# A conformer block on one core: every background matmul moved into the attention's 64x64 tiles

## The chip, the cores and the metric

The kernel runs on one core of a Trainium2 chip. The metric is the device time of one execution in microseconds. Its profile comes from one further execution, taken by the hardware profiler. The engines are PE (TensorE), ACT (ScalarE), DVE (VectorE), POOL (GpSimd) and SP (SyncE, which here only issues DMAs).

## The reference

Two sequences of 4000 tokens with 144 features pass through one conformer block: a feed-forward layer with residual, attention with 4 heads of 36 features, a gated convolution over 5 tokens, a second feed-forward layer and a last layer norm. All inputs and the output are bfloat16.

```python
h = _silu(_layernorm(x) @ w_ff1a) @ w_ff1b          # 144 -> 576 -> 144
x = x + 0.5 * h
qkv = _layernorm(x) @ w_qkv                         # 144 -> 432, 4 heads of 36
p = _softmax(einsum('bhqd,bhkd->bhqk', q, k) * 36 ** -0.5)
x = x + einsum('bhqk,bhkd->bhqd', p, v) @ w_o
h = _layernorm(x) @ w_pw1                           # 144 -> 288
h = h[..., :144] * _sigmoid(h[..., 144:])
x = x + _silu(depthwise_conv5(h, dw)) @ w_pw2
x = x + 0.5 * (_silu(_layernorm(x) @ w_ff2a) @ w_ff2b)
return _layernorm(x)
```

## The kernel before

**Work and tiles.** The 8000 tokens are 16 chunks of 500 (8 for each sequence), a chunk is four blocks of 125 tokens. Attention goes over phases (a chunk of queries) and key tiles of 64: 1008 pairs of chunk and tile for the four heads. For each pair four QK matmuls fill the array at once (64 rows x 64 columns each: the two heads of a pair on the two partition halves, the two pairs side by side) and write 2 x 500 columns in two PSUM banks. The exponential turns them into probabilities PT: on ACT in one instruction of 1000 columns, or, for 190 of the pairs, on DVE in five instructions ("DVE tile"). Four PV matmuls (64 rows x 37 columns; the 37th column sums the probabilities) add into PSUM banks 6 and 7. QK and PV matmuls are all in tiles of 64x64.

**Background.** Everything else is called background and runs between the attention's instructions: layer norms (statistics on DVE, power and scaling on POOL), transposes of a normalized chunk (through DRAM by DMA, from `XN` to `rows` to `XT` or `XTQ`; in the head and the tail on PE), the feed-forward layers (`ff`, `ff_tile`, `ff_part`, weights `WA`, `WE`, `WB`), projections to Q, K and V (`proj`, `vproj`), the output projection (`WO`), the gate (`glu`, `glu_left`, weights `WP1`, `WPZ`), the convolution as matmuls with diagonal matrices (`conv`, `DG`) and its projection (`WP2`). These matmuls use the whole array: 144 features are 128 rows and a second slice of 16 rows padded to 80 (72 and 72 for `XTQ`). Outside the tail silu is computed as tanh on ACT (tile `TH`) and a product on DVE, so that the exponential's table can stay loaded.

**Banks.** Banks 0 to 5 serve QK pairs and the background, one bank at a time for the background; 6 and 7 collect PV.

**What sets the order.** A recording layer (`Rec`, `Sched`) writes all instructions down engine by engine. Generators stand for the chains of background work; `pick` chooses what comes next by costs and due times (`POLICY`, one value for every 21 pairs). After that `reorder` shifts blocks of each engine by a table (`ORDER`), and `PLACES` gives the PSUM banks. What is left is a fixed order on every engine, with semaphore waits. Matmuls carry a `kind` ("q" for the attention's tiles, "f" for full ones); the planner charges a fixed time where the kind changes. In the head, where PE would pause, `Rec.op` inserts matmuls on the identity matrix (`warm`, as many as `FILLS` says) beside the 50 at the start.

**Head and tail.** In the head chunk 0 is taken in two halves (`pre_first`) with weights loaded from ACT's and SP's queues; the last three chunks are finished after the last exponential (`mode["tail"]`), again in halves, with the silu table loaded.

The helper that issues every instruction is at line 419, so all rows of the profile name L419 and are told apart by their tiles.

Of the kernel before, what the change touches and what calls it, by code (L numbers as in the profile page):

```python
# [12 lines left out]
D = 144  # L13
H = 4
DH = 36
HD = 72
ML = 128
LC = 16
LP = 80
# [5 lines left out]
CW = 502  # L25
# [9 lines left out]
FILLS = (5, 2, 5, 12, 3, 1, 3) + (0,) * 60  # L35

# [3 lines left out]
        "PPPPPPPPQOPPPPROQNPPQRPQLPPRPTPUPNIZOVOKVVL~OOKOK~OUHINSNLMMMOPNOJSOOL[I[KMYMKOGRNJHFKOOOE^NNN_dMKLM"  # L40
        "nXMJ@LJMFMYGaJNKMJhLLLLljKKKKKKWKMMWNKK`BJJJQRecHFSIGKH]QKMRGKPMJJMMQTNPNXTRSUJUJJJSLPMPPQUQQNKOTOOR"
        "OQLPPPPPYOOPN[NNNOMfRNLYULMIMOS^KIMOJNaNNQMNHPPaUOMQNYKPSPPQUSVV^QQ^_Q5<@QCPMKIMNNTQMSMNSNUOYQKMMOQQ"
        "^MSOORNOPPCOORPZP^O]OOO[OCNOQEHMUJNNTOMR[MQWXMPMMNNDMPXSNNZMMTMMMTMPLMPP]OOOOQQNUKNOMQMP]WNOMPNVKYPN"
        "JNQHNOOPQQQMPPQOPUP]MNNNOOTNNOMNWOPPMPNOW]VNN[MMHMKYMMQ]YKI`JLQYJJKV[KHMJTLJOJPMQORPVMQNYMN]MN[bLLLL"
        "LMNLPRPKWOYFMNOVNOHXXMKOLNNNN[[_MMMTLLTKKKLJOOPRP`MO_OMNOMPQLLMRMMMPPPQOSYP[MOOISOLNPPIPSPTOLRNNWPNO"
        "QQMMPUQRN[QQQRJFPPPPJQQSPPKQQNPPPPVPPQOPVXOOPNDNPRROSVSYNFWMPYUPNDPJFPNPTOPYOLOPNQ[NLNRPMRLNNOPhUNZM"
        "MMNLNNPMMWYLPNZKNLMF[LPPSLVINLNOMWQNYPYPLQHKOSNORPGPPPS[OOLOOPPYLNNNVOMNOM^QMNTOO_KMMNOMPPLPNQOYL]RY"
        "LMKLMMPLY]KLNNQXMRXSLI[MDObNOENPMMNSNNQMMWNNNOSVNiKZNNQOTFNNOMXXUMMMM?TLLIYMQXXLLMMQZMJJ`ORLMUMKQYNL"
        "INPMMUVNLNOMYPMOORNNRUNKPNO_ROQLSSKMQMKPROLPSOORNOSOOOTVNNNNSNTMTMNNOVXNOMORLSNVXIMSYLMKLN^XYNLMNHMM"
        "WLLMXMNYMOLNNXMNXMMVMM[SLJLLZN^OLNNJUbLLLQNLPRGNNOOOPNRNOPPPeOOOOPSOOORROf`OPNO^@QDLJLMOLTKLTMTRKGMQ"  # L50
        "QNUOPNROYYPZOHNbILLLLbTLLSLLLLPLM_M[MMMMMcMMMMNLMOdZMNNNNIMMMMXMNNVOMKMMZNOUaMMMQMM]^HOMKNNNJZMKM[LM"
        "QgLLLMWMMMMU]LLLV^MQJMWTMHBHMZSKL[PLLZTMK_bMMIGbMPLPQMSVCKRKSMBINPPSPVOLOOOOZQNNS[MMMMNSMOMNO]aNNcMM"
        "MMMMMMNLNNNZWNZMZPNKPMYBENOPJYNNPMPQOLQNPPRRO[YQJNOPQOPXFPHPNOOOPWOOOOOOXPMTQOLOK^OXNNOMPPPLPPHQQNgR"
        "cOLQOMPNOOOOdRM@LdOJOIPIOOOJOOOOJOOPNUPNOOQQYLQ]NLZ[LLLdWKIKLLLWULE]LLLLLOMWRcKLLLNZM[PMMRILNKZJ`[JK"
        "MOLLUbKeJLLYKOUKMMMMMY=KMNNZNL^NLNNNNNN_NNNOQQNPTHNN_NLOOO^QMNPKO^QQM_JFPLOPJMNPPLPhMPROOPQOWOWNNNNU"
        "U?NO[HMTOOOCNOOOQO[OQOUOOOPHVORPYMGNPPMOVNN[QOVKPNZPGLOY]OPLOPPPBHOOORPRROR`OPWQNZCLNNPQZKMQETOJOMNU"
        "OOOOOPPPP[OOPNQNQRLMVZLOTNKPLLOOPPVPNOVOMRMOSLOOPPPPPZOWOMNNN]NLMPRTLNZUNLQMNYWNRAOPTOSHRNDQOPTOOPNP"
        "UOUQ_LROQQIQFNOYPNUKQNKTNKOQRSTNQNRXFQOQVQULMVEMPPP[PPPQODZcMPMMQINPKMPNOOOPRMNPPPQOZOOOOOQOMOOPXOOZ"
        "NNNNNN`NPWMXNNOPNKOCNOXPNOQOMZQMUOKXMZP[^XIMMOOKPABPJOPPPXOOQOPPPRIOPSOVSMOTKQUKLPNQNPXQOMROMPMQWQMU"
        "OQNJMQQNPQQTQOKTNO[NQOPQOUOOVRMUZPNVSYMN`OQK6TNNZ;NLNVMMMMTMMVWMMdMNLMNOO]N[MMM]XLJKKRK^aJHNPPRKNX>N"  # L60
        "OJLOMNPPPSPPQTVOOQVPLPQOAPQOPQOQZVOLOMRUMKL[MPMOOQWMMNNYOLNORNNNOYVNNNOWLMMROORROH]QNQMNOXNOMPMUPKMY"
        "NTOLORSTJMWOPPFObTYLNQSMKG_MKMNN`RMKLOLR]MKPNgIMMMNOYNKNNNNNZTMQXILIXJLMQLYOSJMNPU_]JLOKRSMMHLMOMQOW"
        "OOQOMOUNPNUQRM`YYLOREKNKKV[LJNLOSQJN`KPXLObLMWNK]MIJQLLOUO^LDLTKQNLVLQ^MMQRMSFMUWMNNWMG^MTRMJYLRPNGO"
# [2083 lines left out]
```

## Time and profile before

| | us |
|---|---|
| median of two runs | 875.17 (874.74 and 875.6) |
| span of the profiled execution | 873.9 |
| first exponential starts | 19.38 |
| silu table loaded for the tail | 838.61 |

The profiled execution's span runs from its first to its last instruction; what lies around it is not in it. Matmuls are pipelined, so PE's busy share counts each one's whole length through the array and is not a measure of how much more would fit. "Idle before" in a group's row is idle time of that engine just ahead of these instructions, with what ended it.

### The profile page before, as it was taken

To read this page: it belongs to the slowest core of one execution; us is meant where nothing else is said; L and a number is where in the kernel's file an instruction comes from. 1 tells how busy PE (TensorE), PEld (TensorE's weight loads), DVE (VectorE), ACT (ScalarE), POOL (GpSimd) and SP (SyncE) were. 2 spreads that over 40 slices of the span, in tenths; PEclk is the share of its full clock that TensorE was granted. 3 is DMA by queue.
4 is the path that set the end of the run, shared out by engine and by line. 5 is a ranking of instruction groups with operands and counts; after the bars stand their busy time and mean duration, and the time that the engine had idled before them with its cause. 6 is when DMAs were issued, how large, how long until landed. Compare 5 with 4: busy or idle time off the path is not lost.

```text
span 873.9 us, 27051 instructions
## 1 busy us (share of the span) xinstructions
PE 844.3 (97%) x11419; PEld 385.8 (44%) x11419; DVE 824.8 (94%) x1821; ACT 845.4 (97%) x1098; POOL 292.8 (34%) x573
## 2 busy tenths in 40 slices
PE   8999999999999999999999999999999999999996
PEld 6543444334444434443444444445444433444465
DVE  7988999999999999999989999899999999999987
ACT  6799999999999999999999999999999999999985
POOL 6750350341325141152211552621314413022434
PEclk9999999999999999999999999999999999999999
DMA  4230101121121020212001120110111011001111
GB/s 100 49 62 29 23 17 44 33 67 30 29 52 39 17 50 11 45 22 47 23 4 29 24 56 17 30 30 16 37 31 24 21 31 21 19 15 38 28 26 35
DMA packets 114353, 28.82 MB, mean 33 GB/s; under 512 B 101090, under 2 KB 114230, under 8 KB 114230
## 3 DMA queue, kind: packets, MB, share of 16 engines
q1 hardware_dynamic: 112646, 26.39, 13.8%
q8 instruction: 90, 1.47, 0.7%
q10 hardware_dynamic: 1584, 0.69, 0.3%
q14 instruction: 33, 0.27, 0.1%
HBM read 13.44 MB, written 13.61 MB: 31 GB/s over the span
## 4 chain that ended last, share of the span: by engine, by line
ACT 59%; PE 25%; DVE 11%; POOL 4%; issue 1%; POOLq 0%; DVEq 0%
ACT PT L419 54%; PE PS L419 25%; ACT TH L419 5%; DVE PT L419 4%; POOL XN L419 2%; POOL RS L419 2%; DVE ST L419 2%; DVE X L419 1%; DVE XN L419 1%; DVE HT L419 1%; DVE U L419 0%; DVE KT L419 0%; DVE RS L419 0%; DVE AN L419 0%; DVE XT L419 0%
## 5 line engine op out<-in xcount | busy, mean ns | idle before, releaser
L419 ACT ACTIVATE PT<-PS 128x1000 bf16<-128x1000 f32 (+1 forms) x818 | 752.0, 1051 | 3.7 <-PE PS L419 2.8
L419 PE MATMUL PS<-QT,KT 64*64 64x500 bf16 x3968 | 419.9, 384 | 12.4 <-ACT PT L419 7.4
L419 PE MATMUL PS<-PT,VA 64*37 64x500 bf16 x4728 | 406.4, 372 | 1.6 <-DVE QT L419 1.0
L419 DVE TENSOR_SCALAR PT<-PS 128x500 int16<-128x500 f32 x380 | 250.2, 668 | 6.9 <-PE PS L419 5.1
L419 PEld LDWEIGHTS PS<-QT,KT 64*64 64x64 bf16 x3968 | 124.8, 104 | 232.0 <-ACT PT L419 132.2
L419 POOL TENSOR_SCALAR RS<-ST 125x4 f32<-125x4 f32 x130 | 37.8, 291 | 475.6 <-DVE ST L419 469.0
L419 PEld LDWEIGHTS PS<-PT,VA 64*37 64x37 bf16 x4728 | 142.7, 96 | 93.4 <-issue 13.6
L419 DVE TENSOR_SCALAR PT<-PT 128x1000 uint16<-128x1000 uint16 x380 | 154.2, 419 | 2.3 <-PE PS L419 1.0
L419 POOL TENSOR_SCALAR XN<-X,RS 125x144 bf16<-125x144 bf16 x260 | 144.7, 586 | 9.7 <-DMA out_dram<-XN 1.5
L419 DVE TENSOR_TENSOR PT<-PT 128x1000 bf16<-128x1000 bf16 x190 | 127.5, 674 | 0.9
L419 ACT ACTIVATE TH<-PS 128x500 bf16<-128x500 f32 (+3 forms) x194 | 102.8, 551 | 4.7 <-PE PS L419 4.5
L419 POOL TENSOR_TENSOR RS<-RS,NHALF 125x4 f32<-125x4 f32 (+1 forms) x93 | 92.8, 1002 | 33.5 <-DVE RS L419 27.9
L419 DVE SCALAR_TENSOR_TENSOR HT<-TH,PS 128x500 bf16<-128x500 bf16 (+1 forms) x135 | 81.0, 613 | 10.1 <-ACT TH L419 9.7
L419 PE MATMUL PS<-XT,WA 80*128 80x500 bf16 (+5 forms) x288 | 74.5, 364 | 4.2 <-DVE XT L419 1.0
L419 DVE BATCH_NORM_STATS2 ST<-X 125x6 f32<-125x288 bf16 x160 | 65.5, 446 | 1.6 <-DMA X<-in_x_dram 1.4
L419 DVE SCALAR_TENSOR_TENSOR X<-PS,X 125x288 bf16<-125x288 f32 (+1 forms) x128 | 56.6, 449 | 5.6 <-PE PS L419 4.3
L419 PE MATMUL PS<-WB,HT 128*125 128x144 bf16 (+1 forms) x640 | 52.6, 230 | 0.8 <-ACT HT L419 0.5
L419 PEld LDWEIGHTS PS<-WB,HT 128*125 128x125 bf16 (+1 forms) x640 | 44.3, 136 | 14.2 <-issue 4.3
L419 PEld LDWEIGHTS PS<-XT,WA 128*128 128x128 bf16 (+1 forms) x288 | 21.1, 97 | 37.7 <-issue 10.1
L419 POOL COPY U<-U 128x2 bf16<-128x2 bf16 (+1 forms) x54 | 12.0, 263 | 56.2 <-DVE U L419 56.2
L419 DVE STREAM_TRANSPOSE XN<-XN 128x320 f32<-128x320 f32 x54 | 27.0, 500 | 2.8 <-POOL XN L419 2.6
L419 PE MATMUL PS<-U,DG 128*128 128x250 bf16 (+6 forms) x204 | 28.8, 263 | 0.1
(95 smaller groups left out, 519.9 us busy)
## 6 DMA issues: line engine op xcount, KB each, us to landing
rows<-XN SPq DMA_DIRECT2D x216, 40.0 KB, 2.0
XT<-rows SPq DMA_DIRECT2D x56, 128.0 KB, 2.0
rows<-AN SPq DMA_DIRECT2D x60, 40.0 KB, 2.0
X<-in_x_dram SPq DMA_DIRECT2D x15, 140.6 KB
XTQ<-rows SPq DMA_DIRECT2D x26, 70.3 KB
out_dram<-XN SPq DMA_DIRECT2D x13, 140.6 KB
XT<-rows SPq DMA_DIRECT2D x56, 16.0 KB, 1.9
out_dram<-XN SPq DMA_DIRECT2D x3, 70.3 KB
```

Of the source, the lines that this page charges most:

```text
L419: ins = getattr(eng, o.name)(*o.a, **o.k)
```

## The change

Every background matmul except three kinds (the float32 transposes of the attention's output, those with `KL`, and the warm-up) is written as matmuls of at most 64 rows and 64 output columns.

- **144 features are three slices of 48 rows**, and they lie twice in SBUF, on partitions 0 to 47 and 64 to 111 (`KS`, `NS`, `HF`). The two copies are the two lanes `r` of the array. Weights are loaded in that form: `load_a` and `load_b` issue two DMAs for each weight, `load_heads` loads `WQ` and `WK` head by head, eight DMAs, in place of one load of `WQKV` and copies on POOL. `WE`, `HT5` and most zero fills are gone.
- **Lanes and banks.** Lane 0 and lane 1 write into different banks (but for V and the leftover channels, where they share one). `Couple` and `Pair` take two banks at once. `residual` works on all four blocks of a chunk in one go (two blocks a lane), and one DVE instruction of 576 columns adds them to X in place of two of 288.
- **`lane_run`**: outside head and tail a background step of one lane (two matmuls) goes together with one half of a PV step on the other lane (`partner`, `emit_O`).
- **Transposes** on PE are done by halves of 64 columns (`spread`), three slices, and copied in one instruction of 750 columns for two blocks; by DMA they are read back twice, once for each partition half. `XTQ` is a ring of five chunks in place of eight.
- The fillers and `FILLS` are gone; the 50 matmuls at the start stay.
- `POLICY`, `FJ`, `ORDER` and `PLACES` have new values. 194 pairs go to DVE (190 before), 798 + 16 to ACT (802 + 16).

The core of the diff:

```diff
-LP = 80
+HF = 64
+KS = 48
+NS = 3
-FILLS = (5, 2, 5, 12, 3, 1, 3) + (0,) * 60
+def c_q(n, ways=4):
+    return (n / 2400 + 0.0028) / ways
...
-        if eng == "pe" and self.filler is not None and not self.filling:
...
+class Couple:
+    def take(self):
+        return self.banks.take(), self.banks.take()
...
+    def load_a(eng, q, W, wa, nm, lat=None):
+        for r in range(2):
+            n0, n1 = r * 5 * HF, min((r + 1) * 5 * HF, FF)
+            load(eng, q, W[HF * r:HF * r + KS, :, 0:n1 - n0], by_slice(wa)[:, :, n0:n1], [(nm, "a", r)], lat=lat)
...
-    load_ff("act", "w0", "w3", WA1, WE1, WB1, w_ff1a, w_ff1b, "W1", 3.5, 4.5)
-    load("act", "w1", WQKV[0:HD, :, :], kh(w_qkv), ["WQKV"], lat=5.0)
+    load_a("act", "w0", WA1, w_ff1a, "W1", 3.5)
+    load_b("act", "w3", WB1, w_ff1b, "W1", 4.5)
+    load_heads("act", "w1", WK, D, "WK", 5.0)
+    load_heads("act", "w1", WQ, 0, "WQ", 5.0)
...
+    def lane_run(r, steps, per):
+        for x in range(0, len(steps), per):
+            group = steps[x:x + per]
+            if x:
+                yield need("pe", dur=0.215, kind="q", hold=True)
+            m = None if alone() else partner(1 - r)
+            for y, quads in enumerate(group):
+                for out, l, rh, start, stop, rk, bk, cols in quads:
+                    op("pe", "matmul", out, lhsT=l, rhs=rh, start=start, stop=stop, ...)
+                if y == 0 and m is not None:
+                    emit_O(m, (1 - r,))
...
+        def mm(i, r, a, b):
+            j = i % 2 * TB
+            return [(HT[HF * r:HF * r + HF, h, t, j + a:j + min(b, TB)], WB[HF * r:HF * r + HF, t, :]) for t in range(9)]
+        yield from residual(c, range(NB), mm, 0.5 if silu else 0.25, [("HT", h), (nm, "b", 0), (nm, "b", 1)])
...
     "pe": (
-        "PPPPPPPPQOPPPPROQNPPQRPQLPPRPTPUPNIZOVOKVVL~OOKOK~OUHINSNLMMMOPNOJSOOL[I[KMYMKOGRNJHFKOOOE^NNN_dMKLM"
+        'PPPPPQSNOOPPPPPPQRNOPPPPPPPP`OOVOMXNLoLrKK~OSK^JJJLLLMOMIJLLPKKKMMM[LLRTJJLrHcIJbKKUKKKLQKKKFJMMJLgKPNLf[LMKfjJJJJ[J`IIIdHHIjHiJaFMGBFVGJPFi'
```

What the new order makes of two places. First PE in the middle, at the gate and the output projection of a chunk (WP and XT: the gate; WO and XT: the output projection; QT,KT and PT,VA: the attention's QK and PV). Before:

```order
L419 MATMUL PS<-PT,VA 37x500 x2
L419 MATMUL PS<-XT,WP 128x500 x2
L419 MATMUL PS<-QT,KT 64x500 x4
L419 MATMUL PS<-PT,VA 37x500 x4
L419 MATMUL PS<-QT,KT 64x500 x6
```

After:

```order
L388 MATMUL PS<-XT,WP 64x500 x2
L388 MATMUL PS<-PT,VA 37x500 x6
L388 MATMUL PS<-QT,KT 64x500 x4
L388 MATMUL PS<-PT,VA 37x500 x4
L388 MATMUL PS<-XT,WP 64x500 x2
L388 MATMUL PS<-PT,VA 37x500 x2
L388 MATMUL PS<-XT,WP 64x500 x2
L388 MATMUL PS<-PT,VA 37x500 x2
```

Two full matmuls on 128 columns stood in one run between attention matmuls; six on 64 columns now stand in three runs, each followed by PV matmuls, and the last two runs have PV matmuls between them.

Second ACT at the program's head (WA, WE, WB: weights of the first feed-forward layer; WQKV, WK, WQ, WV: of the projections; DUM: the first use of the loaded table; HT: silu). Before:

```order
L419 DMA WA<-in_w_ff1a_dram 128x512
L419 DMA WA<-in_w_ff1a_dram 16x512
L419 DMA WE<-in_w_ff1a_dram 128x64
L419 DMA WE<-in_w_ff1a_dram 16x64
L419 DMA WB<-in_w_ff1b_dram 128x4x144
L419 DMA WB<-in_w_ff1b_dram 64x144 x2
L419 DMA WQKV<-in_w_qkv_dram 72x2x432
L419 ACT_TABLE_LOAD
L419 ACTIVATE DUM<-NHALF 128x1
L419 ACTIVATE XT<-PS 128x2x125
```

After:

```order
L388 DMA WA<-in_w_ff1a_dram 48x3x320
L388 DMA WA<-in_w_ff1a_dram 48x3x256
L388 DMA WB<-in_w_ff1b_dram 64x9x144 x2
L388 DMA WK<-in_w_qkv_dram 48x3x36 x4
L388 DMA WQ<-in_w_qkv_dram 48x3x36 x4
L388 DMA WV<-in_w_qkv_dram 48x3x72 x2
L388 ACT_TABLE_LOAD
L388 ACTIVATE DUM<-NHALF 128x1
L388 ACTIVATE HT<-PS 128x2x125 x5
```

Eight issues stood ahead of the table load, fourteen stand there now, and the copies to XT that came first after it are no longer on ACT.

1085 lines of the change are left out of this document (595 added, 490 removed), and 89 rows, old and new, of the table POLICY.

## The prediction, made before the changed kernel was run

> **What bounds the kernel now.** I read the page first, for the engines' busy time and the chain that ended last, then the stretches, then who waited for whom, and at the end single rows of the timeline for the spacing of instructions.
>
> ```profile
> span 873.9 us, 27051 instructions
> PE 844.3 (97%) x11419; PEld 385.8 (44%) x11419; DVE 824.8 (94%) x1821; ACT 845.4 (97%) x1098; POOL 292.8 (34%) x573
> ACT 59%; PE 25%; DVE 11%; POOL 4%; issue 1%; POOLq 0%; DVEq 0%
> ```
>
> Three engines look full, so the stretches must say which one decides where. The columns are the stretch, its length, and busy time (and instructions) of PE, weight loads, DVE, ACT and POOL, then the granted clock.
>
> ```profile
> 0.00:25.00 25.00, 20.34 (x236) 15.67 (x237) 19.84 (x75) 16.67 (x33) 17.05 (x42) 1.00 0.38 93
> 25.00:50.00 25.00, 24.41 (x240) 13.70 (x238) 23.90 (x60) 20.09 (x37) 16.75 (x36) 1.00 0.23 49
> 50.00:100.00 50.00, 49.29 (x706) 20.70 (x707) 42.83 (x87) 49.97 (x62) 15.83 (x32) 1.00 0.17 38
> 100.00:200.00 100.00, 97.38 (x1341) 39.51 (x1334) 98.13 (x218) 98.45 (x121) 30.84 (x52) 1.00 0.18 39
> 200.00:400.00 200.00, 197.91 (x2756) 85.66 (x2752) 193.20 (x409) 199.22 (x244) 68.52 (x135) 1.00 0.16 34
> 400.00:600.00 200.00, 194.92 (x2642) 87.43 (x2641) 187.07 (x390) 198.99 (x254) 60.07 (x118) 1.00 0.13 28
> 600.00:800.00 200.00, 193.56 (x2677) 83.36 (x2675) 194.63 (x407) 199.94 (x246) 58.35 (x112) 1.00 0.11 24
> 800.00:838.00 38.00, 37.67 (x523) 15.86 (x516) 35.29 (x76) 37.99 (x49) 13.02 (x31) 1.00 0.14 31
> 838.00:874.00 36.00, 28.82 (x334) 23.88 (x332) 29.88 (x105) 24.12 (x61) 12.40 (x21) 0.95 0.12 31
> ```
>
> From 50 to 838 us ACT is busy for 784.6 of 788 us: idle 3.4 us in all. Its other idle time is 8.3 us up to 25 us, 4.9 us from 25 to 50, where PE is the full engine (24.41 of 25), and 11.9 us in the tail after 838. So ACT sets the end, and a change to PE alone can return only what ACT loses to PE.
>
> ```profile
> ACT TH L419 <- PE PS L419: 4.5, 9, 1.4
> ACT PT L419 <- PE PS L419: 2.8, 8, 0.8
> PE PS L419 <- ACT PT L419: 8.3, 30, 0.5
> ```
>
> These are engine, what waited for whom, us in total, times, longest. ACT's exponentials (PT) visibly wait for PE only 2.8 us; PE waits longer for ACT than that. Waits below the view's resolution must be read from spacings.
>
> ```profile
> 299.84 3.69 ACT L419 ACTIVATE PT<-PS 128x1000 bf16<-128x1000 f32 x4
> 303.86 2.85 ACT L419 ACTIVATE PT<-PS 128x1000 bf16<-128x1000 f32 x3
> 828.94 2.90 ACT L419 ACTIVATE PT<-PS 128x1000 bf16<-128x1000 f32 x3
> 832.12 2.94 ACT L419 ACTIVATE PT<-PS 128x1000 bf16<-128x1000 f32 x3
> L419 ACT ACTIVATE PT<-PS 128x1000 bf16<-128x1000 f32 x802 | 743.8, 1059 | 3.7 <-PE PS L419 2.8
> L419 ACT ACTIVATE TH<-PS 128x500 bf16<-128x500 f32 x136 | 83.1, 630 | 3.7 <-PE PS L419 3.6
> L419 ACT ACTIVATE TH<-PS 128x250 bf16<-128x250 f32 x29 | 12.7, 438 | 0.9 <-PE PS L419 0.8
> ```
>
> One exponential lasts 1.06 us, four together 3.69: the next starts 0.88 us after the last, an overlap of 0.18. Three should take 2.82; the three groups took 2.85, 2.90 and 2.94, 0.23 more, or 0.018 for each of 13 exponentials with the group of four. Over 802 that is an estimated 14 us of small lateness hidden inside "busy".
>
> **PE: what the change takes off it.** Matmuls in 64x64 tiles run four at a time; the rows for the prices:
>
> ```profile
> 300.04 0.38 PE L419 MATMUL PS<-QT,KT 64*64 64x500 bf16 x4
> 300.36 0.84 PE L419 MATMUL PS<-WB,HT 128*125 128x144 bf16 x10
> 301.12 0.61 PE L419 MATMUL PS<-QT,KT 64*64 64x500 bf16 x6
> 302.44 0.62 PE L419 MATMUL PS<-XT,WP 128*128 128x500 bf16 x2
> 303.59 0.73 PE L419 MATMUL PS<-IDF,QT 128*125 128x128 f32 x4
> 835.59 1.01 PE L419 MATMUL PS<-PT,VA 64*37 64x500 bf16 x16
> 18.35 0.65 PE L419 MATMUL PS<-WQKV,XTQ 72*64 72x72 bf16 x28
> ```
>
> Sixteen PV matmuls are four rounds: 1.01 less the 0.38 of one round's length, over three, is 0.21 a round, 0.0525 for each matmul. A 500-wide full matmul costs 0.62 - 0.38 = 0.24, a 144-wide one about 0.07 (0.84/10 less its end). After the QK round at 300.04 the array is free at 300.25, and the full matmuls start at 300.36: a change of kind costs about 0.11. The order has 775 such changes before and 103 after (96 of them around KL and the float32 transposes).
>
> Before: 8,760 attention matmuls x 0.0525 = 460; background 404 x 0.24, 896 x 0.07, some 290 x 0.12 (250-wide), 345 narrower ones about 26, V 512 x 0.023 = 12, transposes of IDF 128 x 0.18 = 23, warm-up 9, together about 265; changes 775 x 0.11 = 85. Sum 810, 93% of the span. After: 8,808 x 0.0525 = 462; tiles 540 x 0.0525, 1,770 x 0.026, 3,072 x 0.0175, 796 x 0.014, 672 that run two at a time x 0.028, V 768 x 0.023, IDF 23, warm-up 5.5, together about 204; changes 103 x 0.11 = 11. Sum 677, 78%. So PE has some 130 us less to do and stops being close to a bound. None of this is itself time off the end.
>
> **ACT.** Its own work: exponentials 802 to 798 (four tiles more go to DVE), -4 x 0.88 = -3.5. Spacing of 500-wide operations is 0.63 - 0.18 = 0.45, of 250-wide 0.44 - 0.18 = 0.26; I take 0.665 for 750 wide and 0.17 for 125. Tanh: five 500-wide and one 250-wide fewer, -2.5. Silu on HT: 16 500-wide fewer, 32 250-wide and 10 125-wide more, +2.8. Copies to XT: 20 x 0.26 become 9 x 0.665, +0.8; to XTQ -0.3. Small copies about +1. Sum -2 us. Bounds -3.5 (only the exponentials) to 0.
>
> **The middle, 50 to 838.** Recoverable at most 3.4 visible and 14 hidden. I take half, -9: no view says which share of the hidden part is PE's, and waits for a DVE result stay. Bounds 0 and -17.
>
> **DVE** is the next engine. A DVE tile costs its groups' busy time over 190 tiles:
>
> ```profile
> L419 DVE TENSOR_SCALAR PT<-PS 128x500 int16<-128x500 f32 x380 | 250.2, 668 | 6.9 <-PE PS L419 5.1
> L419 DVE TENSOR_SCALAR PT<-PT 128x1000 uint16<-128x1000 uint16 x380 | 154.2, 419 | 2.3 <-PE PS L419 1.0
> L419 DVE TENSOR_TENSOR PT<-PT 128x1000 bf16<-128x1000 bf16 x190 | 127.5, 674 | 0.9
> L419 DVE SCALAR_TENSOR_TENSOR X<-PS,X 125x288 bf16<-125x288 f32 x126 | 55.8, 450 | 5.6 <-PE PS L419 4.3
> ```
>
> (250.2 + 154.2 + 127.5)/190 = 2.8, four more are +11.2. Residual adds: 126 x 0.443 = 55.8 become 18 x 0.443 and 54 of twice the width; from 288 wide (0.443) and 500 wide (250.2/380 = 0.658) I extend to 0.735 at 576, together 47.7, -8.1. Four gating products fewer, -2.6. About +1, against 49 us of idle time on DVE: cost nothing at the end. If that cover were gone it would be 1 us.
>
> **The head.** The first silu waits for ACT's queue, which issues weight DMAs first:
>
> ```profile
> 0.74 0.90 ACTq L419 DMA_DIRECT2D WA<-in_w_ff1a_dram  x2
> 4.32 0.80 ACTq L419 DMA_DIRECT2D WQKV<-in_w_qkv_dram  x1
> 5.14 1.28 ACT L419 ACT_TABLE_LOAD   x1 [5.14 <-DVE RS L419]
> 8.77 2.30 ACT L419 ACTIVATE HT<-PS 128x500 bf16<-128x500 f32 x5 [0.17 <-PE PS L419]
> 21.65 2.65 SPq L419 DMA_DIRECT2D rows<-XN  x4
> ```
>
> Eight issues end at 5.1; now fourteen stand there, twelve of them over 48 partitions, which no row shows. The nearest: 0.45 (WA, 128 and 16 partitions), 0.66 (rows, 64), 0.80 (WQKV, 72). Fourteen take 6.3 to 11.2, with 0.74 ahead and table load and its first use (1.5) behind: first silu possible at 8.5 to 13.4, against 8.77. Between 0.45 and 0.66, 0.53 gives 9.7: +1; bounds 0 and +4.7. The same width matters on SP, where each transposed chunk is read back by two or four such DMAs; 110 XT issues at up to 0.66 instead of 112 at WA's 0.45 delay chunks by under half a microsecond each, behind queued chunks, at nothing. Thirty-one filler matmuls go from the head. The clock stood at 1.00 there and at 0.95 in the tail, where PE pauses, so it can fall; +0 to +2, taken as 0. By the Trainium skill (TensorE: Matmul & The Clock Gate, Part 1), an idle window of about 3.4 us halves the clock; by that rule three steps of the head like the ten matmuls of 0.84 would take 0.7 longer each, an estimated 2 us, and no run here shows the head without fillers.
>
> In 25 to 50 us PE was full and ACT idle 4.9: -3, bounds 0 and -4.9. **The tail**: 36 us with no engine above 30 busy, a chain of short steps; its PE part shrinks with the changes of kind, while the wider copies to XT lengthen it: -1.5, bounds -4 and +1.
>
> **Sum**: 873.9 - 2 - 9 + 1 - 3 - 1.5 = 859.4. The profiled run lies 1.3 under the median of the runs, 875.17; as a run, 861.
>
> **Rivals.**
> *More than that (0.24).* All the lateness was PE's: -2 - 17.4 - 4.9 - 4 and nothing lost in the head, so 845.6, as a run 847. For it speaks the tight pairing of ACT and PE; against it that PE waited for ACT 8.3 us and ACT's exponentials for PE 2.8.
> *Nothing (0.18).* The hidden lateness is ACT's own or DVE's, head and tail cancel: 874.
> *A new wait on PE (0.10), slower.* The order now puts PV matmuls inside background work at 224 places (2 before), so that one lane of the array serves each. PE works in order: a PV matmul whose probabilities are not ready holds the background behind it, and the next QK, for which ACT waits. PE's waits for ACT above were 8.3/30 = 0.28 us each; at half of that, 0.14 at each place, 224 x 0.14 = +31 replaces the -9: 899, as a run 901. It decides above 0.10 us a place.
> *Short matmuls pay for their own weight load (0.03), slower.* Loads of 64 columns last 104 ns:
>
> ```profile
> L419 PEld LDWEIGHTS PS<-QT,KT 64*64 64x64 bf16 x3968 | 124.8, 104 | 232.0 <-ACT PT L419 132.2 <-DVE PT L419 23.4 <-issue 17.1
> ```
>
> If none is hidden, 7,600 background matmuls add 7,600 x 0.104/4 = 198 to PE's 677: 875, and with the head and tail idle of before (4.7 + 7.2) and waits 890 to 900. Against it: 28 V matmuls with 64-column loads took 0.65 together, though 14 in a row on one tile would need 14 x 0.104 = 1.46 for loads alone. The Trainium skill (TensorE: Matmul & The Clock Gate, Part 3) says that loads overlap running matmuls only where the row group differs; those 28 share their rows and overlap all the same, so the trace speaks against the rule for this case.
>
> **The numbers.** Forecast 861 has 0.45, with a range of its own of 853 to 869 (middle and tail varied by half of their bounds); the rivals 0.24, 0.18, 0.10, 0.03. Two per cent, about what a measurement of this kernel can tell from no change, is 17.5 us: 857.7 and 892.7. Faster: 0.24 and a quarter of the forecast's range, 0.35. Slower: 0.13. Same: 0.52. The range for 8 in 10 runs from 845 (847 with ACT's own work at its bound of -3.5 in place of -2) to 884: the no-change case with the upper bounds of head, fillers and tail, 874 + 3.7 + 2 + 1 and 3 for DVE's chains.
>
> **What would show it.** Right: PE's busy share falls well below 97% while ACT's stays at 99% from 50 to 838; ACT in 25 to 50 above 22; three exponentials in 2.82 to 2.86; first silu at 9 to 10. Wrong: ACT below 98% in the middle with "ACT PT <- PE PS" in the tens of us, which is one of the slower cases (PE waiting in front of PV for the first, PE full for the second); a first silu beyond 12; or a clock under 1 in the head.

## The result and the profile after

| | before | after |
|---|---|---|
| median of the runs, us | 875.17 | 952.28 (950.49 and 954.07) |
| span of the profiled execution | 873.9 | 952.1 |
| first exponential starts | 19.38 | 25.30 |
| first exponential's start to the last one's end | 818.2 | 876.0 |
| from there to the end | 36.4 | 50.7 |

The changed kernel is slower: the ratio is 1.0883 (95% interval 1.0832 to 1.0933), where 861 and a gain had been forecast. Of the 78.2 us in the profiled executions 5.9 lie in the head, 57.8 between the exponentials, 14.4 in the tail. The page of the changed kernel, its span, its engines' busy time and its chain of waits:

```profile
span 952.1 us, 37428 instructions
PE 835.2 (88%) x16632; PEld 434.2 (46%) x16632; DVE 836.8 (88%) x1778; ACT 861.7 (91%) x1104; POOL 287.3 (30%) x557
ACT 34%; DVE 27%; PE 24%; DMA 6%; SPq 3%; issue 2%; POOL 2%; ACTq 1%; POOLq 0%; DVEq 0%
```

No engine is full from end to end any more. ACT's share of the chain fell from 59% to 34%, and DVE (27%), DMA (6%) and SP's queue (3%) stand where it was: each of them holds the chain up in turn. The stretches of the changed kernel, columns as before (length; PE, weight loads, DVE, ACT, POOL; the clock):

```profile
0.00:25.00 25.00, 18.89 (x492) 15.80 (x492) 20.17 (x69) 12.75 (x29) 13.56 (x31) 0.93 0.48 108
25.00:50.00 25.00, 19.98 (x616) 15.03 (x616) 20.35 (x50) 17.59 (x31) 13.65 (x26) 0.93 0.32 74
50.00:100.00 50.00, 40.30 (x998) 22.61 (x990) 29.07 (x57) 42.47 (x56) 17.99 (x37) 0.97 0.24 57
200.00:400.00 200.00, 184.34 (x3572) 94.32 (x3564) 189.21 (x385) 187.71 (x230) 61.55 (x122) 1.00 0.22 48
400.00:600.00 200.00, 179.85 (x3225) 87.18 (x3225) 180.21 (x361) 191.84 (x234) 56.16 (x106) 0.99 0.14 32
600.00:800.00 200.00, 177.82 (x3038) 81.60 (x3033) 174.42 (x347) 195.91 (x236) 41.93 (x79) 1.00 0.13 30
901.00:952.00 51.00, 36.37 (x1346) 30.36 (x1338) 33.17 (x110) 26.87 (x72) 16.39 (x31) 0.87 0.12 32
```

From 200 to 400 us ACT is idle for 12.3 of 200 us (0.8 before), from 600 to 800 for 4.1 (0.1). PE has idle time too, 15.7 and 22.2 us there, so over these stretches it is not short of time, and ACT has to wait all the same. Who waits for whom (engine, what waited for whom, us, times, longest):

```profile
ACT PT L388 <- PE PS L388: 31.9, 60, 3.0
ACT TH L388 <- PE PS L388: 14.1, 21, 3.7
PE PS L388 <- ACT PT L388: 37.0, 116, 1.0
PE PS L388 <- DMA XT<-rows: 6.4, 5, 2.4
PE PS L388 <- DMA XTQ<-rows: 5.7, 5, 2.2
PE PS L388 <- issue: 4.9, 6, 1.4
```

ACT's exponentials wait for PE 31.9 us (2.8 before), and PE waits for ACT's exponentials 37.0 us (8.3 before). The page's rows of PE tell in front of which matmuls it stands idle (busy time, mean ns of one, then the idle time ahead of them and what ended most of it); the kernel before, then the changed one:

```profile
L419 PE MATMUL PS<-QT,KT 64*64 64x500 bf16 x3968 | 419.9, 384 | 12.4 <-ACT PT L419 7.4
L419 PE MATMUL PS<-PT,VA 64*37 64x500 bf16 x4728 | 406.4, 372 | 1.6 <-DVE QT L419 1.0
L388 PE MATMUL PS<-QT,KT 64*64 64x500 bf16 x3968 | 449.1, 384 | 62.8 <-ACT PT L388 31.0
L388 PE MATMUL PS<-PT,VA 64*37 64x500 bf16 x4744 | 479.6, 373 | 6.7 <-ACT PT L388 3.4
```

31.0 of the 37.0 us stand in front of QK matmuls. These read nothing that an exponential writes; what they can wait for is a bank whose scores an exponential still reads. So PE and ACT wait for each other by turns, and PE's part of it is for banks. Not all of this wait comes from the new use of the banks: a PE with less to do arrives sooner and waits longer, 17.2 us for exponentials in run 5 below, which leaves the banks as they were. Rows of the timeline show one such turn, and two prices of the head and the tail:

```profile
0.73 0.90 ACTq L388 DMA_DIRECT2D WA<-in_w_ff1a_dram  x2
7.38 0.94 ACTq L388 DMA_DIRECT2D WV<-in_w_qkv_dram  x2
9.76 2.44 ACT L388 ACTIVATE HT<-PS 128x250 bf16<-128x250 f32 x9
21.55 0.80 ACT L388 ACTIVATE XTQ<-PS 128x750 bf16<-128x750 bf16 x1 [1.19 <-PE PS L388]
24.14 0.65 ACT L388 ACTIVATE QT<-PS 128x250 bf16<-128x250 f32 x2 [1.80 <-PE PS L388]
25.30 1.00 ACT L388 ACTIVATE PT<-PS 128x1000 bf16<-128x1000 f32 x1
...
886.64 1.00 ACT L388 ACTIVATE PT<-PS 128x1000 bf16<-128x1000 f32 x1 [0.56 <-PE PS L388]
887.09 0.32 PE L388 MATMUL PS<-WP,SW 64*64 64x144 bf16 x8
887.70 0.60 PE L388 MATMUL PS<-QT,KT 64*64 64x500 bf16 x6
887.71 0.76 DVE L388 SCALAR_TENSOR_TENSOR X<-PS,X 125x576 bf16<-125x576 f32 x1
888.15 1.00 ACT L388 ACTIVATE PT<-PS 128x1000 bf16<-128x1000 f32 x1 [0.51 <-PE PS L388]
...
922.03 0.73 PE L388 MATMUL PS<-WB,HT 64*64 64x144 bf16 x36
```

The turn at 886.64: the program gives the banks. The convolution's projection (WP,SW) writes two of the six banks at 887.09 and holds them until DVE has added them to X (887.71 to 888.47). Two others hold the scores that ACT reads from 886.64 to 887.64. A DVE tile has the fifth until 887.62; the sixth is empty, but an exponential takes two neighbouring banks (`take_pair`). Only then, at 887.70, can the next QK matmuls write, and the next exponential starts at 888.15, 1.51 after the last instead of 0.88.

How often banks are crowded: I matched the trace's instructions with the program's order, which names each one's bank. Background and DVE tiles together held three or more of the six banks around 54 of 806 exponentials on ACT before (50 to 838 us), and around 127 of 806 after (50 to 900). Those 127 came 0.31 us late each, the other 679 0.087; before, the others came 0.035 late. (Late is a start measured from 0.18 before the end of ACT's work ahead of it.) The sum of it is 31 us before and 98 after: some 34 of the 67 more lie on the exponentials with crowded banks, 33 are spread over the others. The counts hang on what "around" takes in (at the exponentials' starts alone they are 29 and 82), and they show that lateness and crowded banks go together, not that one makes the other. By the same matching DVE tiles hold 0.67 of the six banks on average before and after, and background 0.96 before and 1.12 after; the banks of a residual add are held for 1.34 us before, one at a time, and 1.84 after, two at a time.

### The profile page after: what moved, and what is told of

Read it like the earlier page. It is cut to its first block, busy times and chain, and to the rows that moved or that the text cites. A ratio compares the mean times of both kernels' runs of the same rounds, so it can differ in the third digit from the quotient of the medians.

```text
span 952.1 us, 37428 instructions
## 1 busy us (share of the span) xinstructions
PE 835.2 (88%) x16632; PEld 434.2 (46%) x16632; DVE 836.8 (88%) x1778; ACT 861.7 (91%) x1104; POOL 287.3 (30%) x557
## 2 busy tenths in 40 slices
DMA packets 128373, 39.52 MB, mean 42 GB/s; under 512 B 107171, under 2 KB 128212, under 8 KB 128212
## 4 chain that ended last, share of the span: by engine, by line
ACT 34%; DVE 27%; PE 24%; DMA 6%; SPq 3%; issue 2%; POOL 2%; ACTq 1%; POOLq 0%; DVEq 0%
ACT PT L388 30%; PE PS L388 24%; DVE PT L388 15%; SPq L388 3%; ACT TH L388 3%; DMA rows<-XN 2%; DVE X L388 2%; DVE HT L388 2%; DMA XT<-rows 2%; DVE ST L388 2%; DVE XN L388 2%; DVE QT L388 1%; POOL XN L388 1%; DMA XTQ<-rows 1%; POOL RS L388 1%
## 5 line engine op out<-in xcount | busy, mean ns | idle before, releaser
L388 ACT ACTIVATE PT<-PS 128x1000 bf16<-128x1000 f32 x814 | 751.3, 1014 | 36.0 <-PE PS L388 31.9
L388 PE MATMUL PS<-QT,KT 64*64 64x500 bf16 x3968 | 449.1, 384 | 62.8 <-ACT PT L388 31.0
L388 PE MATMUL PS<-PT,VA 64*37 64x500 bf16 x4744 | 479.6, 373 | 6.7 <-ACT PT L388 3.4
L388 DVE TENSOR_SCALAR PT<-PS 128x500 int16<-128x500 f32 x388 | 253.5, 670 | 18.5 <-PE PS L388 17.4
L388 PE MATMUL PS<-XT,WA 48*64 48x250 bf16 (+2 forms) x1998 | 110.8, 266 | 14.4 <-DMA XT<-rows 5.3
L388 POOL TENSOR_TENSOR RS<-RS,NHALF 125x4 f32<-125x4 f32 (+2 forms) x95 | 89.8, 949 | 52.6 <-DVE RS L388 47.1
L388 PEld LDWEIGHTS PS<-XT,WA 48*64 48x64 bf16 x1998 | 72.6, 109 | 41.2 <-DVE HT L388 9.3
L388 DVE SCALAR_TENSOR_TENSOR X<-PS,X 125x576 bf16<-125x576 f32 (+1 forms) x74 | 49.7, 674 | 27.9 <-PE PS L388 26.8
L388 DVE BATCH_NORM_STATS2 ST<-X 125x6 f32<-125x288 bf16 (+1 forms) x160 | 65.7, 447 | 0.7 <-DMA X<-in_x_dram 0.3
L388 PE MATMUL PS<-WB,HT 64*64 64x144 bf16 (+1 forms) x2304 | 46.7, 233 | 3.3 <-issue 2.1
L388 PEld LDWEIGHTS PS<-WB,HT 64*64 64x64 bf16 (+1 forms) x2304 | 41.4, 112 | 8.7 <-issue 2.7
L388 PE MATMUL PS<-XT,WP 48*64 48x500 bf16 (+1 forms) x204 | 33.1, 374 | 0.2
```

The costliest lines, as they stand in the source:

```text
L388: ins = getattr(eng, o.name)(*o.a, **o.k)
```

## The experiments

Fourteen runs, each timed in three rounds beside the kernel before, whose median was 874.8 to 875.6 in them. "Head" is the start of the first exponential in the profiled execution, "middle" from there to the last one's end, "tail" from there to the end of the span.

| run | kernel | median | ratio (95%) | head | middle | tail |
|---|---|---|---|---|---|---|
| | before | 875.17 | 1 | 19.4 | 818.2 | 36.4 |
| | after | 952.28 | 1.0883 (1.0832–1.0933) | 25.3 | 876.0 | 50.7 |
| 1 | after, recorded plan only | 948.44 | 1.0841 (1.0809–1.0873) | 24.2 | 871.7 | 50.0 |
| 2 | before, recorded plan only | 898.35 | 1.0267 (1.0252–1.0283) | 20.8 | 835.4 | 40.5 |
| 3 | run 1 without `partner` | 965.75 | 1.1034 (1.1000–1.1068) | 27.0 | 864.0 | 71.7 |
| 4 | after with fillers | 950.62 | 1.0864 (1.0831–1.0897) | 24.1 | 872.9 | 51.5 |
| 5 | before, PE 100 us lighter | 877.56 | 1.0022 (1.0009–1.0036) | 18.5 | 819.1 | 35.7 |
| 6 | after, PE 90 us lighter | 951.66 | 1.0896 (1.0844–1.0948) | 25.1 | 873.9 | 50.9 |
| 7 | before, read back twice | 884.11 | 1.0100 (1.0085–1.0115) | 18.6 | 826.4 | 36.5 |
| 8 | run 2, `KEEP` 1 | 954.20 | 1.0908 (1.0889–1.0926) | 20.6 | 883.0 | 43.9 |
| 9 | run 1, `KEEP` 2 | 986.93 | 1.1267 (1.1247–1.1288) | 27.7 | 869.5 | 89.1 |
| 10 | run 2, `AHEAD` 0.6 | 925.92 | 1.0578 (1.0560–1.0596) | 20.8 | 857.0 | 46.9 |
| 11 | run 10, `KEEP` 1 | 943.88 | 1.0783 (1.0766–1.0801) | 22.9 | 874.6 | 45.3 |
| 12 | run 1, other `POLICY` | 936.50 | 1.0686 (1.0658–1.0714) | 26.2 | 871.8 | 38.5 |
| 13 | run 11, read back twice | 960.32 | 1.0973 (1.0942–1.1004) | 20.6 | 894.7 | 46.1 |
| 14 | run 1, `AHEAD` 0.6 | 968.88 | 1.1070 (1.1052–1.1089) | 27.0 | 878.7 | 65.4 |

**Runs 1 and 2: is it the tables?** `ORDER` and `PLACES` are worked out for one program; emptying them leaves the order that the planner recorded.

```diff
-ORDER = {
-    "pe": (
...
+ORDER = {"pe": "", "act": "", "dve": "", "pool": "", "sp": ""}
+PLACES = ""
```

> The changed kernel with its ORDER and PLACES tables left empty: every engine runs the order that the planner recorded, and banks are those that the planner chose. Theory 1 (the order, not the tiles, loses the time, and the tables are part of it): faster than the changed kernel's 952 by 8 to 25 us, 927 to 944, with less PE waiting for transfers (XT, XTQ: 12.1 us now). Theory 2 (the tiles themselves lose it, the tables repair a part as such tables should): slower than 952, 955 to 980.

> The kernel before with its ORDER and PLACES tables left empty. It gives the value of the old tables and, beside the first run, the difference of the two recorded plans. If its tables were worth 8 to 20 us, 883 to 895. Theory 1 then sees part of the 77 us between the kernels in the tables and the rest, 40 to 55, between the recorded plans; if both plans without tables lie within 20 us, the tables are the whole loss.

Without tables the kernel before loses 898.35 - 874.98 = 23.4 us (874.98 is its median beside these runs) and the kernel after gains 3.8, about what its two executions differ (950.49 and 954.07). Run 1 came out between its two expected ranges, run 2 above its range. So the old table was worth 23.4 and the new one nothing; but 50.1 of the 77.1 us stand between the recorded plans, where no table is. By place, in the profiled executions of runs 1 and 2, the difference is 49.2 us: 3.3 in the head, 36.3 in the middle and 9.5 in the tail.

**Run 3: does PE wait in front of the PV matmuls that stand in background work?** That was the slower rival of the prediction.

```diff
-        "DUET": (
-            1, 1, 1, 1, 1, 1, 1, 1, 1, 1, 1, 1, 1, 1, 1, 1, 1, 1, 1, 1, 1, 1, 1, 1, 1, 1, 1, 1, 1, 1, 1, 1, 1, 1, 1, 1, 1,
...
+        "DUET": (0,) * 49,
```

> The first run with DUET set to 0 for all pairs: no PV matmul is put inside a background step any more, a background step of one lane runs without a partner. The rival of the prediction (PV matmuls inside background hold PE at 224 places) expects a gain against the first run, up to 31 us. Theory 1 (background that waits for banks and products holds PE, the PV matmuls there are ready) expects a loss of 5 to 25 us, since the lanes then run half empty.

Leaving the pairing out costs 17.3 us, and all of it lies in head and tail: the middle is 7.8 us shorter than in run 1, the tail 21.7 longer. So this run does not price the pairing; the other plan left more for the tail, and run 14 shows that one unrelated value moves this kernel by 20.4. What speaks against the rival is the row of the PV matmuls above: all 4744 of them together kept PE idle for 6.7 us (1.6 before), where the rival needed 31.

**Run 4: the clock.** Filler matmuls put back into PE's pauses of head and tail.

```diff
+        if eng == "pe" and self.filler is not None and not self.filling:
+            n = int((ready - max(start, self.filler_free()) - 0.3) / 0.112)
...
+                for _ in range(n):
+                    self.filler()
...
+    R.filler = warm
```

> The changed kernel, tables as they are, with matmuls on the identity put back into PE's planned pauses before the first exponential and in the tail (bank 7), half of each pause. Theory 3 (the lost fillers let the clock fall: 0.66 from 20 to 25 us, 0.5 from 940 to 950) expects the clock at 1.0 in these stretches and 4 to 12 us less, 940 to 948. If the clock there costs nothing on the path, 952 within 2.

The clock of the changed kernel in two stretches:

```profile
20.00:25.00 5.00, 3.91 (x112) 3.43 (x112) 3.60 (x12) 1.80 (x5) 3.13 (x6) 0.66 0.55 120
940.00:950.00 10.00, 6.43 (x192) 5.76 (x192) 4.75 (x16) 4.03 (x13) 2.02 (x3) 0.50 0.11 30
```

And of run 4:

```profile
20.00:25.00 5.00, 4.34 (x166) 3.33 (x164) 4.95 (x17) 3.42 (x9) 3.98 (x8) 1.00 0.57 120
940.00:948.00 8.00, 2.47 (x120) 1.94 (x109) 2.75 (x9) 2.63 (x9) 1.39 (x2) 0.92 0.13 36
```

The fillers bring 0.66 to 1.00 and 0.50 to 0.92, and the time falls by 1.7 us, which is within both intervals. The low clock is there; what it is worth cannot be told from nothing here, and it is little of the 77. It is not what made the tail 14.4 longer: in this run's profiled execution the tail still took 51.5.

**Runs 5 and 6: what is PE's load worth?** The accumulating background matmuls write an eighth of their columns, so their results are incomplete; instructions, banks and waits stay. Run 5 (1,252 matmuls, some 100 us of PE by the prediction's prices); run 6 does it to 5,560 of the tile form, some 90 us.

```diff
+        if name == "matmul" and kind == "f" and not k["start"]:
+            n = k["rhs"].shape[-1] // 8
+            if n > 1:
...
```

> The kernel before, order and tables untouched. 1252 full background matmuls, those that add to a sum already begun, take only an eighth of their columns, so that PE has some 100 us less to do (at one column per 1/2.4 ns); the background's results are wrong by that, nothing else changes. The prediction's theory (PE's fullness costs ACT half of its lateness; less PE work comes back at the end) expects 861 to 866. Theory 1 (the order is fixed, ACT sets the end, PE's spare time stays idle) expects 869 to 874.

> The changed kernel, order and tables untouched. 5560 background matmuls in tiles, those that add to a sum already begun, take an eighth of their columns, some 90 us of four-tile time less on PE; the background's results are wrong by that. If PE working ahead of a late QK is what holds ACT in the new order, 930 to 944. If ACT there waits only for banks, products and transfers that no faster PE brings earlier, 947 to 952.

The time falls in neither. Run 5 even came out above both of its expected ranges, 2.1 us over the kernel before (877.56 and 875.5). Two of its stretches:

```profile
25.00:50.00 25.00, 21.32 (x228) 14.13 (x226) 22.79 (x57) 18.59 (x34) 16.08 (x34) 0.78 0.22 47
200.00:400.00 200.00, 190.86 (x2768) 82.31 (x2772) 194.01 (x411) 199.28 (x246) 67.76 (x132) 1.00 0.16 34
```

From 200 to 400 ACT is as full as before, 199.28 us for 199.22, and PE's busy share fell only from 197.91 to 190.86. On the chain of waits PE's share fell from 25% to 8% and ACT's rose from 59% to 70%. The order is the same as before, so each exponential can be found again in both traces. The first starts at 19.38 before and at 18.54 in run 5, the 81st at 117.06 and 119.89, the last at 836.97 and 837.00. So run 5 loses 3.7 us up to the 81st and gets 2.8 back behind it. Where it loses, the granted clock is down, 0.78 from 25 to 50 for 1.00 before; behind 100 us it is 1.00 until the tail. The ten executions point the same way: 873.55 and 875.20 us at a mean clock of 0.986, 880.01 at 0.972. So PE's load was worth something in the middle, 2.8 us of the 17.4 that the prediction saw there, and the head took it back; that the lower clock alone did this was not isolated. The rest of the lateness between exponentials stayed with 100 us less on PE. The same stretches of run 6:

```profile
25.00:50.00 25.00, 21.86 (x634) 16.20 (x632) 20.53 (x49) 18.40 (x32) 14.25 (x28) 0.50 0.30 65
200.00:400.00 200.00, 176.05 (x3614) 85.40 (x3614) 190.53 (x390) 188.28 (x231) 60.90 (x122) 1.00 0.22 49
```

Here ACT stays at 188.28 (187.71 in the changed kernel). From 25 to 50 the clock fell to 0.50. From 200 to 400 it was 1.00. By the same comparison run 6 is 2.7 us behind the changed kernel at the 151st exponential (216.14 and 213.41) and 2.5 ahead at the 791st (873.73 and 876.18): some 5 us back, where two executions of the changed kernel differ by 3.6, and nothing at the end (951.66; 952.28 without the edit).

**Run 7: the second read-back alone.** In the kernel before every transposed chunk is read from `rows` once more, into a DRAM buffer that nobody uses: 56 DMAs of 128 KB, 26 of 70 KB.

```diff
+    DD = nc.dram_tensor("twice", [NXT + 2 * CPB, 128, 2, 128], F32).ap()
...
+                                (DD[s, :, :, :], 0, 128, 128, 0.0, 0.0)], f"t{s}", wk)
```

> The kernel before, order and tables untouched, but behind each read-back of a transposed chunk SP issues more of it again, into DRAM, on the same queue, and the readers wait for that too: one DMA of 128 KB more for each XT (56), two of 70 KB for each XTQ (13). That is the change's second copy in bytes, and somewhat more in issues. The prediction (read-backs at nothing) expects 875 within 3. If the second copy is what delays the chunks, 880 to 895.

It costs 8.6 us (884.11 - 875.5 beside it). Run 7's DMA issues and its waits of PE:

```profile
twice<-rows SPq DMA_DIRECT2D x56, 128.0 KB, 2.4
```

```profile
PE PS L419 <- DMA twice<-rows: 6.5, 9, 2.4
```

PE waits 6.5 us for chunks whose last read-back is this new one. Most of the loss falls in one place: the 21st exponential starts 0.2 us later than before (59.86 and 59.61), the 31st 5.3 (75.79 and 70.49), and between them PE stands idle 2.44 us at a time for such a chunk. So the price hangs on where in the order a late chunk falls. In the changed kernel the read-backs are larger and land later than before (us at the end of the row; the same tile before was `XT<-rows` of 128.0 KB at 2.0):

```profile
XT<-rows SPq DMA_DIRECT2D x110, 144.0 KB, 2.9
XTQ<-rows SPq DMA_DIRECT2D x52, 70.3 KB, 2.1
```

The 12.1 us for which PE waits on these two (6.4 and 5.7, above; no such row before) are of the kind that run 7 made. What they cost at the end in the tile form was not measured by itself.

**Runs 8 to 11: banks.** `KEEP` is the number of bank pairs that the planner keeps for QK while it places background. It was 2; after, 16 of the 49 stretches (among them 8 to 20) have 1, since a step that takes two banks finds no room otherwise. Run 8 sets 1 in the kernel before, run 9 sets 2 in the kernel after.

```diff
-    KEEP = 2
+    KEEP = 1
```

> The kernel before with empty tables (898.35 in the second run) and one number changed: the planner keeps one pair of neighbouring banks free for QK instead of two (KEEP 1 for 2), as the changed kernel's POLICY does for 16 of its first 21 stretches of 21 pairs. All matmuls are those of before. Theory 4 (the six banks: with one pair for QK, a QK waits for the exponential that reads its banks and the exponential waits for that QK, in turn) expects 925 to 960, with PE's waits for ACT PT in the tens of us (8.1 now). If banks are not scarce, 890 to 910.

> The changed kernel with empty tables (948.44 in the first run) and KEEP 2 for all pairs. Theory 4 expects no gain: ACT's exponentials wait less for PE in the stretch up to 400 us, but background that needs two banks at once is put off, so the time comes back as late keys in the first 150 us and as a longer tail: 950 to 985. If the low KEEP is only a bad choice of the planner's table, 905 to 935.

Run 8 loses 55.9 us against run 2. Two of its waits:

```profile
ACT PT L328 <- PE PS L328: 33.4, 65, 1.6
PE PS L328 <- ACT PT L328: 11.9, 41, 0.6
```

ACT's wait came as in the changed kernel (33.4; 31.9 there). PE's wait for ACT, for which tens of us had been expected, stayed at 11.9. Run 9, just above its expected range, shows that `KEEP` 1 was no blunder of the plan: with 2, the tile form loses 38.5 more, since its two-bank steps are left over; the tail of the profiled execution grows from 50.0 to 89.1. Its middle is only 2.3 us shorter than run 1's.

But any disturbance moves a plan. As a control, run 10 changes a value that does not say how many banks are kept (`AHEAD`, how long before ACT's end PE turns to the next QK), and run 11 adds `KEEP` 1 to it.

```diff
-        "AHEAD": (
-            0.5, 0.5, 0.5, 0.7, 0.7, 0.7, 0.5, 0.5, 0.7, 0.6, 0.6, 0.6, 0.6, 0.6, 0.6, 0.6,
...
+        "AHEAD": (0.6,) * 49,
...
-    KEEP = 2
+    KEEP = 1
```

> A control for the run with KEEP 1. The kernel before with empty tables (898.35) and another of the planner's tables made coarse: AHEAD, by how much background must end ahead of ACT's queue, 0.6 for all stretches in place of 0.5 to 0.85; banks are kept as before. It shows what any disturbance of a tuned table costs. If a disturbance costs little, 895 to 905, and the 56 us of KEEP 1 are the banks'. If it costs much, 910 to 930, and only what KEEP 1 costs beyond it is the banks'.

> The control with KEEP 1 beside it: the effect of KEEP alone, on a plan whose tuning is gone already. Theory 4 (banks) expects 15 to 45 us over the control; if KEEP 1 cost only by its disturbance, within 8 us of the control.

The control alone costs 27.6 us, so half of run 8's loss may be nothing but a plan thrown out of tune. On the same footing `KEEP` 1 costs 943.88 - 925.92 = 18.0. How much of this is disturbance once more is not known, since no second value without a bearing on banks was changed on top of run 10. ACT's exponentials wait 19.7 us for PE in the control already, and 31.0 in run 11. The middle of run 10, and below it of run 11:

```profile
200.00:400.00 200.00, 196.56 (x2611) 80.00 (x2600) 192.97 (x406) 189.56 (x233) 59.73 (x120) 1.00 0.16 34
```

```profile
200.00:400.00 200.00, 197.25 (x2582) 83.46 (x2582) 188.84 (x401) 181.49 (x230) 73.86 (x142) 1.00 0.16 34
```

ACT falls from 189.56 to 181.49 with one pair fewer kept, while PE's row barely moves.

**Runs 12 and 14: is the new plan only badly tuned?** Run 14 gives the kernel after the control's disturbance; run 12 changes 102 values of its `POLICY` (`AHEAD` 1.2 from the 27th stretch on, `MAXQ` 1 from the 37th, `KEEP` 1 and `DUET` 0 in the 45th to the 49th, and others).

```diff
-            0.6, 0.6, 0.56, 0.56, 0.56, 0.56, 0.6, 0.5, 0.5, 0.6, 0.6, 0.5, 0.5, 0.5, 0.6, 0.6, 0.6, 0.6, 0.7, 0.7, 0.7,
+            0.6, 0.6, 0.56, 0.56, 1.2, 1.2, 1.2, 1.2, 1.2, 1.2, 1.2, 1.2, 1.2, 1.2, 1.2, 1.2, 1.2, 1.2, 1.2, 1.2, 1.2,
...
```

> The first run (changed kernel, empty tables, 948.44) with other values in POLICY, found by changing a value or a stretch of values at a time and keeping what shortens the plan; 102 of the values differ, most of them behind the pair 750 and in the tail, KEEP in seven. All matmuls, transfers and lanes are those of the change. If lost tuning is the whole difference of the recorded plans (50 us), 895 to 915. If the two-bank steps and the second read-backs set a floor that no values lift, 920 to 945.

> The first run (changed kernel, empty tables, 948.44) with AHEAD 0.6 for all stretches, the same control as on the kernel before (27.6 us there). If the changed kernel's plan is as well tuned as the old one, 965 to 980. If it is out of tune already, 945 to 958.

Run 12 gains 11.9 us, and the profiled execution puts it in one place: the tail takes 38.5 us instead of run 1's 50.0, the stretch between the exponentials 871.8 instead of 871.7. Run 2's tail was 40.5. So the longer tail is mostly the plan's choice of what to leave for last. Of the middle the run says less, since most of the changed values belong to its last part. Run 14 loses 20.4, so by this one value the new plan was nearly as well in tune as the old one, which loses 27.6.

**Run 13: both causes in the old matmuls.** Run 11 and run 7's extra read-backs together, with every background matmul still in its full form.

> The kernel before, matmuls on the whole array as ever, with the three things put together that cost time one by one: coarse AHEAD (a plan out of tune) and KEEP 1, which gave 943.88, and the second read-back, which gave 8.6 us on the kernel before. If they add, 948 to 958, the changed kernel's 948 to 952 without a single background tile. If the read-back hides behind the other waits, 942 to 947.

960.32, just above the expected 948 to 958: 16.4 more than run 11, twice of what the read-backs cost in the tuned kernel. Run 13's waits and its chain:

```profile
ACT PT L328 <- PE PS L328: 39.7, 65, 2.7
PE PS L328 <- DMA twice<-rows: 12.9, 18, 1.7
```

```profile
PE 36%; DVE 24%; ACT 22%; DMA 8%; SPq 5%; POOL 4%; issue 1%; ACTq 0%; POOLq 0%
```

DMA and SP's queue come into the chain as in the changed kernel (8% and 5%; 6% and 3% there), without one tile matmul in the background; PE leads it, with 36% where the changed kernel has 24%. Beside run 14, which has the same `AHEAD`, the medians are near each other, 960.32 and 968.88, but not for the same reason: run 13's middle is 16.0 us longer and its tail 19.4 shorter. So old matmuls with these two handicaps can be as slow as the change; that the change is slow through them is not shown by it.

**The 77.1 us, put together.** Tables: 23.4 that the old one gave and 3.8 that the new one takes, 27.2. Recorded plans: 50.1, by place 3.3 us in the head, 36.3 in the middle and 9.5 in the tail, and run 12 takes the tail's part away with planner values. For the middle there are two candidates whose size was measured on the old matmuls: in the middle one bank pair fewer costs 17.5 us (857.0 to 874.6, runs 10 and 11) and the second read-back 20.1 (874.6 to 894.7, runs 11 and 13). Together that is 37.7, about the 36.3. It remains argued: both stand in for what the tile form does, in a plan out of tune; the two plans with the same disturbance (runs 10 and 14) differ by only 21.6 in the middle; and neither candidate was taken out of the tile form by itself. Each number is the difference of two plans, and one value of `AHEAD` moved a plan by 20 and 28 us.

## Why the prediction was wrong, by its steps

**In short.** The sum went from 873.9 down by terms for lighter engines alone. It gave the new order the old one's fit for nothing, which run 2 puts at 23.4 us; it had no term for steps that hold two banks, and put the second read-back at nothing, which together are the candidates for 36.3 us in the middle; and the gain that it expected there, -9, measured 2.8 in run 5.

**The bound was read rightly.** "ACT sets the end, and a change to PE alone can return only what ACT loses to PE": run 5 took some 100 us off PE, 2.8 came back in the middle, and nothing at the end. This holds for the tuned order; in runs 2 and 10 PE has 48% and 39% of the chain, and what its load is worth in those plans wasn't tried.

**"The middle: I take half, -9", the first step that failed.** The bound itself, 0 to -17, took it as given that the lateness was partly PE's load. Run 5 puts PE's share at 2.8 in the middle, a third of the 9; most of the lateness did not go with PE's load. Whether the rest is waits for banks or for results was not taken apart. The rows had said so (PE waited for ACT longer than ACT's exponentials for PE), and the prediction used that only against its rival "more than that".

**The loss in the middle was never a term.** The prediction's part on PE counted matmuls and changes of kind, its part on DVE the wider residual adds; no line asked how many PSUM banks a step holds, or for how long. `Couple` and `Pair` take two of six where one step took one, and `residual` holds them until one DVE instruction of 576 columns is done. `KEEP` at 1 stood in the new `POLICY`. Run 11 puts one bank pair fewer at 18.0 us on the old matmuls; what the two-bank steps themselves cost is argued from that and from PE's wait in front of QK matmuls (7.4 us before, 31.0 after), not isolated. The Trainium skill (TensorEngine Tiling (Array Packing), Gotcha 1: PSUM Pressure) says that row tiling increases PSUM pressure, since different row tiles write to different banks; it gives no price. The crowded exponentials counted above, 54 before and 127 after, agree with it.

**"at nothing", for the read-backs on SP.** The prediction compared issue times alone, "110 XT issues ... instead of 112". The old 112 were 56 large ones and 56 of 16 KB; the new 110 are all 144 KB. The bytes of all DMAs rose from 28.82 to 39.52 MB, and the landing from 2.0 to 2.9 us. Run 7 measures 8.6 us for a second reading, run 13 16.4, both on the old matmuls.

**What the old order was worth was not priced.** Run 2 gives 23.4 us for the table alone. The prediction's sum started from 873.9 and so kept the old kernel's tuning, as if a plan derived anew for other instructions would be as good; this is the largest part of the loss that an experiment isolates.

**The head, +1.** The step that was priced came out: fourteen issues took 7.59 us (0.73 to 8.32), 0.54 each where 0.53 was taken, and the first silu stood at 9.76 where 9.7 was computed. But the first exponential came 5.9 later, and the chain behind the silu had no term: the projection's QT waits 1.80 us for PE, XTQ 1.19 ahead of it in the same trace. With fillers back it came 1.2 earlier (24.08 in run 4). What the rest is stays open.

**25 to 50, -3.** ACT's busy time there went from 20.09 to 17.59. The step saw a full PE as the reason. In run 5 PE had less to do and ACT was no busier there (18.59), but the clock was down to 0.78, so that run does not settle it.

**Fillers taken as 0, bound +2.** The clock fell, to 0.66 and 0.50; run 4 puts its worth at 1.7 us, not clear of noise. By the Trainium skill (TensorE: Matmul & The Clock Gate, Part 1) an idle window of about 3.4 us halves the clock. The value agrees with the 0.50 here; the idle window does not stand in the traces: in the tail PE's longest pause between 928 and 940 us is 1.50 us, and in run 6 the clock is 0.50 from 20 to 70 us with PE busy for 44.16 of the 50.

**The tail, -1.5, bounds -4 and +1.** It took 14.4 longer, far beyond its bounds. Run 12 shortens run 1's tail by 11.5 with planner values alone, so what failed is that the tail's work was taken as fixed: the plan decides how much background is left for it.

**ACT's own work and DVE's.** The counts were as said (798 and 16 exponentials, 194 DVE tiles). Nine HT of 250 columns took 2.44, 0.25 apart where 0.26 was taken; two XT of 750 took 1.49, 0.69 apart for 0.665; a residual add of 576 took 0.76 for 0.735. These sizes were right and far too small to matter. "DVE +1, hidden" is not what hurt; DVE was asked only for its busy time, while the add's end is also what frees two banks.

**PE, 810 to 677.** A row of four tiles has its price: 36 matmuls at 922.03 are nine rounds, (0.73 - 0.23)/8 = 0.0625 where 0.23 is one's length, and 0.07 was taken. That tiles run four at a time with their loads hidden holds, so that rival falls. The sum itself cannot be read from a busy share, which counts each matmul's whole length; runs 5 and 6 show that little hung on it.

**The rivals.** "More than that" and "nothing" fall with the sign. "A new wait on PE" had the right side, and the mark set for it came (ACT under 98%, "ACT PT <- PE PS" at 31.9), but it was the wrong mechanism: PV matmuls kept PE idle for 6.7 us in all, QK matmuls for 62.8. The marks that the prediction set could tell that PE was late, not why: a bank that is not free and a PV matmul that is not ready both show as PE late. The rows of PE by tile tell them apart.

**What stays open.** No version beat the kernel before. Which part of the 36.3 us in the middle is banks and which is read-backs was not isolated in the tile form. Whether a table worked out for the tile form would win back anything like 23 us wasn't tried, nor a residual that holds its banks for less long, nor what in the head takes the 6 us.

## What to carry to other kernels

Before crediting a lighter engine with time, ask what it shares with the engine that sets the end. Here that was six banks, of which the new form takes two at a time, and with them the room in which PE and ACT work ahead of each other. Making an instruction cheaper in place, as in run 5, is a quick test of what that engine's load is worth; follow one and the same instruction through both traces, since a gain in one place (2.8 us) can hide behind a loss in another (3.7).

A finely tuned static order is itself worth time (23.4 us here), which this change of structure gave up. To compare two structures, compare both without tables and with the same disturbance (runs 10 and 14), and give every suspected cause a control; run 8 alone would have put 55.9 us on what a control leaves at 18.0. Compare by place as well: runs 13 and 14 end near each other with middles 16.0 us apart.

## What was unexpected of the hardware

The granted clock fell where PE was given less to write in the same span: in run 6 it stood at 0.50 from 25 to 50 us, where the changed kernel has 0.93, with nearly the same number of instructions (634 and 616) and an unchanged total; in run 5 at 0.78 for 1.00. It was not so everywhere: from 200 to 400 us it stayed at 1.00 in both. In the head, a PE with less to write was also a PE at a lower clock.

PE stood idle 4.9 us in six places for nothing that the profile shows ("issue"), up to 1.4 us at a time, where the kernel before has no such row for its matmuls. Five of the six lie in the tail, between 914 and 933 us, in front of runs of short matmuls. It is no general slowness of issue: the weight loads' waits of that name fell from 86.2 us to 28.3. What stood behind these six wasn't isolated.
